# Output projection with eleven matmuls a tile in place of twelve, its weights brought into pieces of 128 rows by DMAs

## The chip, the core and the metric

The kernel runs on one core of a Trainium2 chip. The core has engines that run side by side, each with its own order of instructions and semaphores between them: TensorE (PE; its weight loads, PEld, run beside its matmuls), VectorE (DVE), ScalarE (ACT), GpSimd (POOL), and SyncE (SP), which here only issues DMAs. SBUF is the working memory of 128 partitions; PSUM takes what PE writes, in 8 banks of 128 x 512 float32.

The metric is the time of one execution on the device in microseconds, as the median of several runs. Beside it stands one profiled execution, whose trace gives each instruction's start and length.

## The reference

One block of a transformer with two parts, for a sequence of 2048 tokens with 448 channels, in float32. The first part is linear attention with 16 heads of 28 channels, the second an MLP over the tokens. Both are modulated by six vectors made from `c`.

```python
def _A_ref(x, wqkv, wo):
    q, k, v = qkv[0], qkv[1], qkv[2]                  # (x @ wqkv) cut into heads
    phi = lambda t: jnp.where(t > 0, t + 1, jnp.exp(t)) + 1e-6
    pq, pk = phi(q), phi(k)
    kv = jnp.einsum("bhsd,bhse->bhde", pk, v)
    z = jnp.einsum("bhsd->bhd", pk)
    num = jnp.einsum("bhqd,bhde->bhqe", pq, kv)
    den = jnp.einsum("bhqd,bhd->bhq", pq, z)[..., None] + 1e-6
    return (num / den).reshape(B, S, D) @ wo          # after turning the heads back

h = _layernorm(x) * (1 + ca) + sa
x = x + ga * _A_ref(h, A_wqkv, A_wo)
h = _layernorm(x) * (1 + cb) + sb
x = x + gb * _B_ref(h, B_w1, B_b1, B_w2, B_b2)        # W2 gelu(W1 h) over tokens
```

The output projection of the title is `num / den @ wo`. The kernel never forms `num`: it multiplies the masked `kv`, `wo` and `ga` into one 448 x 448 matrix Wp, so that a tile's result is phi(q), divided by its denominators, times Wp.

## The kernel before

The sequence is cut into 16 tiles of 128 tokens (`NT`). Products that must keep float32 accuracy are made from two parts: a value is copied on ACT into a rounded format (float32r; the "high" part) and the rest is subtracted on DVE (the "low" part). A product is then three matmuls, high x high, high x low and low x high. `split` (lines 78 to 80) is this pair of operations.

The kernel has these stages. First k and the outer products of phi(k) with the normalised x are made for all tiles, with some of the q projections between them (`Q_EARLY`: tiles 0 to 4). Then Wp is made (lines 846 to 852). Then comes the loop of lines 856 to 916, which is the stage of the change. Then the rest of the MLP's first matrix product, and the second one.

The loop has NT + LAG = 21 passes. Pass `i` issues, in a pipeline over the tiles:

- on PE: the transposes of tile i (`b_transpose`, line 763), the output projection of tile i-1 (`b_out`, line 776), the q projections that are left (`a_q`, 11 matmuls each; their number a pass stands in `QS`, else one), and from pass 5 on the first MLP product of tile i-5 (`step`, 12 matmuls)
- on ACT and DVE: the high and low part of the turned tile (`b_high`, `b_low`; on the trace pth and ptl), the residual sum of tile i-2 (`b_res`), the scaled phi(q) of tile i+1 (`b_prod`, `b_sum`, `b_recip`, `b_scale`; on the trace pd, den and pn, which the next pass turns), the second layer norm of tiles i-3 and i-4 (y, and the parts h2h and h2l that `step` multiplies), then phi of the q tiles projected in the pass before (`a_phi_q`; eq and rq on ACT, pq on DVE)
- splits of pieces of the first MLP matrix, ahead of their use (`split_to`; on the trace ph and pl from the raw piece pr), and their loads (`load_to`)
- on POOL: the small operations of the layer norm (nm, ny, vw, rt, nb), the addition in the denominators, and the low part of four of the weight pieces as accumulating DMAs (`PIECE_DMA`)

Each engine works in the order in which the program issues to it; nothing is reordered by a planner. A pool of tiles (`slot`, `tslot`, `bank`) makes a new tile wait until an older one in the same place is done with.

The 448 channels of phi(q) are turned in four groups of 112 (`G`, four heads). So Wp, too, lies in four pieces of 112 rows, and PE makes each as the product of a group of `kvm` and a piece of `wo` into a bank (`wp`); `split` makes their parts `Wph` and `Wpl` from there. `b_out` then has four groups with three matmuls each, over 112 rows.

Of the kernel before, what the change touches and what calls it, by code (L numbers as in the profile page):

```python
# [8 lines left out]
F32 = mybir.dt.float32  # L9
F32R = mybir.dt.float32r  # L10
AF = mybir.ActivationFunctionType
# [3 lines left out]
P = 128  # L15
S, D, F = 2048, 448, 1792
NT = S // P
NF = F // P
G = 112
# [15 lines left out]
LAG = 5  # L35
LAST, CUT = 2, 224
MOD_AT = {9: [(4, 0)], 10: [(4, 1)], 11: [(4, 2)], 12: [(4, 3)], 13: [(3, 0)], 14: [(3, 1)]}
QS = {0: 2, 4: 2}
WARM = 9
PRE = 9  # L40
MID = 5
# [6 lines left out]
def block_kernel(ctx: ExitStack, tc: tile.TileContext, x, xt, wqkv, wo, w1, b1, w2, b2, c, wmod, wfirst, out):  # L48
    nc = tc.nc
# [15 lines left out]
    def slot(name, w=D, dt=F32, parts=P):  # L65
        return slots.tile([parts, w], dt, name=name, tag="slot", padded_shape=[P, 512])

    def tslot(name, dt=F32, parts=P, w=D):
        return tok.tile([parts, w], dt, name=name, tag="tok", padded_shape=[P, 512])


    def moving(new, name, dt=F32R, parts=P):
        return new(name, dt=dt, parts=parts, w=512)[:, 16:16 + D]

    def bank(name):
        return psum.tile([P, 512], F32, name=name, tag="bank")

    def split(full, hi, lo):
        nc.scalar.activation(hi, full, AF.Copy)  # L79
        nc.vector.tensor_sub(lo, full, hi.bitcast(F32))  # L80
# [6 lines left out]
    ident = cst.tile([P, P], F32, name="ident")  # L87
# [44 lines left out]
    def load_mod(j):  # L132
        for k in range(4):
            wm[j, k] = (tslot if j == 5 else slot)(f"wm{j}_{k}", parts=G)
            nc.sync.dma_start(wm[j, k], wmod[k * G:(k + 1) * G, j * D:(j + 1) * D])
# [55 lines left out]
    def mod_out(j, ps):  # L191
        mods[j] = cst.tile([P, D], F32, name=f"mod{j}")
        nc.scalar.activation(mods[j], ps[:, :D], AF.Copy, bias=1.0 if j == 4 else 0.0)
# [35 lines left out]
    def mod_part(j, k):  # L229
        if k == 0:  # L230
            macc[j] = (tslot if j == 5 else slot)(f"acc{j}", parts=G)
            nc.vector.tensor_scalar_mul(macc[j], wm[j, 0], sc[:G, 4:5])
        else:
            nc.vector.scalar_tensor_tensor(macc[j], wm[j, k], sc[:G, 4 + k:5 + k], macc[j], op0=ALU.mult, op1=ALU.add)


    def mod_split(j):
        acc = macc.pop(j)
        macc[j] = (moving(slot, f"mh{j}", parts=G), moving(slot, f"ml{j}", parts=G))
        split(acc, *macc[j])  # L240

    def mod_sum2(j):
        ps = bank(f"modp{j}")
        hi, lo = macc.pop(j)
        nc.tensor.matmul(ps[:, :D], ones_r[:G, :], hi, start=True, stop=False)
        nc.tensor.matmul(ps[:, :D], ones_r[:G, :], lo, start=False, stop=True)
        return ps
# [45 lines left out]
    raws, parts = {}, {}  # L293
# [10 lines left out]
    def split_to(i):  # L304
        while done["split"] < min(i, len(pieces)):
            k = done["split"]
            n = pieces[k][3]
            if k in TOKP:
                hi, lo = tslot(f"ph{k}", F32R, w=n * P), tslot(f"pl{k}", F32R, w=n * P)
            else:  # L310
                hi, lo = slot(f"ph{k}", n * P, F32R), slot(f"pl{k}", n * P, F32R)
            if k in PIECE_DMA:
                full = raws.pop(k)
                nc.scalar.activation(hi, full, AF.Copy)
                nc.scalar.activation(lo, hi.bitcast(F32), AF.Copy, scale=-1.0)
                nc.gpsimd.dma_start(lo, full, accum_op=ALU.add)
            else:
                split(raws.pop(k), hi, lo)
            parts[k] = (hi, lo)
            done["split"] += 1  # L320
# [64 lines left out]
    tps = {}  # L385
# [55 lines left out]
    def phi_q(ps, t):  # L441
        dst, e, r = slot(f"pq{t}"), slot(f"eq{t}"), slot(f"rq{t}")
        nc.scalar.activation(e, ps, AF.Exp, scale=mv[t][:, 2:3])
        nc.scalar.activation(r, ps, AF.Relu, scale=mv[t][:, 2:3])
        nc.vector.scalar_tensor_tensor(dst, e, 1.0, r, op0=ALU.min, op1=ALU.add)
        return dst
# [4 lines left out]
    def a_q(t):  # L451
        project(t, 0, "qp")
        qps[t] = close(t, 0)
        del heads[t]

    def a_phi_q(keep=0):
        for t in sorted(qps)[:len(qps) - keep]:
            pq[t] = phi_q(qps.pop(t), t)
# [151 lines left out]
    for t in range(4, NT):  # L610
# [12 lines left out]
        if t == 12:  # L623
            mp = mod_sum2(2)
# [93 lines left out]
    mp = mod_sum2(4)  # L718
    kvb = bank("kvb")
    for ch in range(4):  # L720
        for g in range(4):
            s = slice(g * G, (g + 1) * G)
            nc.tensor.matmul(kvb[:G, s], raw_w[2, ch][:, s], csum[ch][:, s], start=(ch == 0 and g == 0),
                             stop=(ch == 3), skip_group_check=True)
# [4 lines left out]
    mp = mod_sum2(3)  # L729
    load_to(PRE + MID + 3)  # L730
    split_to(8)
    Wph, Wpl = [], []


    H2h, H2l = [None] * NT, [None] * NT
    pns, phs, ys, opb, sums, nms, nm2s, rss, vss = {}, {}, {}, {}, {}, {}, {}, {}, {}
# [11 lines left out]
    def b_eps(t):  # L748
        nc.gpsimd.tensor_scalar_add(dens[t], dens[t], 1e-6)
# [13 lines left out]
    def b_transpose(t):  # L763
        pn = pns.pop(t)
        tps[t] = bank(f"tq{t}")
        for g in range(4):
            nc.tensor.transpose(tps[t][:G, g * P:(g + 1) * P], pn[:, g * G:(g + 1) * G], ident)  # L767

    def b_high(t):
        phs[t] = (slot(f"pth{t}", 512, F32R, parts=G), slot(f"ptl{t}", 512, F32R, parts=G))  # L770
        nc.scalar.activation(phs[t][0], tps[t][:G, :], AF.Copy)  # L771

    def b_low(t):
        nc.vector.tensor_sub(phs[t][1], tps.pop(t)[:G, :], phs[t][0].bitcast(F32))

    def b_out(t):
        ph, pl = phs.pop(t)
        opb[t] = bank(f"op{t}")
        n = 0
        for g in range(4):  # L780
            s = slice(g * P, (g + 1) * P)
            for a, b in ((ph, Wph[g]), (ph, Wpl[g]), (pl, Wph[g])):
                nc.tensor.matmul(opb[t][:, :D], a[:, s], b, start=(n == 0), stop=(n == 11))  # L783
                n += 1

    def b_sums(i):
        if i not in vss:
# [42 lines left out]
    def b_low2(t):  # L830
        nc.vector.tensor_sub(H2l[t], ys.pop(t), H2h[t].bitcast(F32))
# [6 lines left out]
    def step(k, accs, mh, ml, first, last):  # L838
        hi, lo = parts.pop(k)
        for i, ps in enumerate(accs):  # L840
            acc3(ps, hi, lo, slice(i * P, (i + 1) * P), mh, ml, first, last)
# [4 lines left out]
    for g in range(4):  # L846
        wp = bank(f"wp{g}")
        nc.tensor.matmul(wp[:G, :D], kvm[:, g * G:(g + 1) * G], wo_sb[g], start=True, stop=True)
        hi, lo = moving(tslot, f"wph{g}", parts=G), moving(tslot, f"wpl{g}", parts=G)
        split(wp[:G, :D], hi, lo)  # L850
        Wph.append(hi)
        Wpl.append(lo)
    mod_out(3, mp)

    accs, early = None, []
    for i in range(NT + LAG):
        if i == NT - 4:
            load_mod(5)
        if NT - 3 <= i <= NT:
            mod_part(5, i - NT + 3)  # L860
        if i == NT:
            mod_split(5)
        if i < NT:
            b_transpose(i)
        if 0 <= i - 1 < NT:
            b_out(i - 1)
        nq = min(len(late), QS.get(i, 1))
        for _ in range(nq):
            a_q(late.pop(0))
        t = i - LAG  # L870
        mp = mod_sum2(5) if i == NT else None
        if t >= 0:
            if t == 0:
                accs = [bank(f"up{f}") for f in range(4)]
            if i > NT:
                if not early:
                    early = [bank(f"up{W1G[1][0] + f}") for f in range(W1G[1][1])]
                r = i - NT - 1
                step(NT + r, early, H2h[r], H2l[r], r == 0, False)
            step(t, accs, H2h[t], H2l[t], t == 0, t == NT - 1)  # L880
        if mp is not None:
            mod_out(5, mp)
        if i < NT:
            b_high(i)
        scale, res, norm1, norm2 = i + 1 < NT, 0 <= i - 2 < NT, 0 <= i - 3 < NT, 0 <= i - 4 < NT
        if res:
            b_res(i - 2)
        if scale:
            b_prod(i + 1)
        if norm2:  # L890
            b_norm2(i - 4, i)
        if res:
            b_mean1(i - 2, i)
        if norm1:
            b_norm1_a(i - 3)
        if scale:
            b_sum(i + 1)
        if norm1:
            b_norm1_b(i - 3, i)
        if scale:  # L900
            b_eps(i + 1)
        if i < NT:
            b_low(i)
        if norm1:
            b_mean2(i - 3, i)
        if scale:
            b_recip(i + 1)
        if scale:
            b_scale(i + 1)
        if norm2:  # L910
            b_low2(i - 4)
        a_phi_q(nq)
        load_to(14 + (i + 1) // 2)
        split_to(10 + (i + 1) // 2)
        if res or norm1:
            b_rstd(i, 0 if res else 1, 2 if norm1 else 1)

# [248 lines left out]
    for o0, n in W1G[1:]:  # L1166
# [5 lines left out]
        for r in range(first, NT):  # L1172
# [4 lines left out]
            if xleft and k % 2:  # L1177
                t = xleft.pop(0)
# [13 lines left out]
    for n, (kind, p) in enumerate(order):  # L1192
        if jobs:
            jobs.pop(0)()
        while xleft:
            t = xleft.pop(0)
# [73 lines left out]
```

## Time and profile before

| | |
|---|---|
| median of 3 runs | 447.32 us (446.92 to 447.51) |
| profiled execution, whole | 448.35 us |
| its span in the profile | 446.2 us |
| PE busy | 439.1 us, 98% |
| DVE busy | 353.5 us, 79% |
| ACT busy | 267.5 us, 60% |
| POOL busy | 104.3 us, 23% |
| granted clock of PE | 1.0 |
| first transposes of the loop (tile 0) | at 117.43 us |
| last transposes of the loop (tile 15) | at 199.96 us |

How to read its lines: a line of the order of time has the start in us, the length in us, the engine, the line of the kernel, the operation, what it writes and what it reads, the shapes, and the count where several are merged. In brackets stands how long the engine had idled before it and what ended the idle time. PE's matmuls overlap, so what one costs is the distance between two starts, not its length; the same holds to a smaller degree for DVE and ACT. A row of DMAs has the queue that issues, the count, the size of each and the time from issue to landing. `wp`, `op` and `tq` are the banks of Wp's product, of the output projection and of the transposes.

### The profile page before, as it was taken

The numbers are of one execution on the slowest core, as the hardware profiler recorded it, in microseconds if no ns is written. First come the engines' busy times: TensorE is split into PE (matmuls) and PEld (weight loads), VectorE is DVE, ScalarE is ACT, GpSimd is POOL, SyncE is SP. The second block draws the span as 40 slices with busy tenths as digits, with TensorE's granted clock in tenths as the row PEclk, the third lists the DMA queues.
The fourth block names the chain that finished last, engine by engine and source line by source line (L and its number), as shares of the span: only waits on it lengthen the run. The fifth ranks groups of instructions, "written<-read, shape, count | busy, mean of one in ns | idle before, by whom it ended". The sixth has DMA issues, their size and how long they took to land.

```text
span 446.2 us, 7331 instructions
## 1 busy us (share of the span) xinstructions
PE 439.1 (98%) x2370; PEld 405.5 (91%) x2370; DVE 353.5 (79%) x801; ACT 267.5 (60%) x580; POOL 104.3 (23%) x188
## 2 busy tenths in 40 slices
PE   7999999999999999999999999999999999999997
PEld 6878899999899999989999999999999999999996
DVE  3989997689998899896477776649688787978873
ACT  3899877748656876667664345336554546356531
POOL 3227563300025355554300000000110211302101
PEclk9999999999999999999999999999999999999999
DMA  7997999545100004222416453227987569966334
GB/s 236 378 303 165 215 241 229 104 147 181 54 0 1 24 25 114 54 48 47 143 54 217 137 178 127 90 88 228 257 201 194 92 177 214 208 183 110 54 89 62
DMA packets 58853, 63.22 MB, mean 142 GB/s; under 512 B 5248, under 2 KB 49344, under 8 KB 58816
## 3 DMA queue, kind: packets, MB, share of 16 engines
q1 hardware_dynamic: 51616, 51.17, 38.0%
q0 software_dynamic: 7200, 11.60, 16.4%
q8 instruction: 18, 0.29, 0.3%
q14 instruction: 19, 0.16, 0.1%
HBM read 46.57 MB, written 7.34 MB: 121 GB/s over the span
## 4 chain that ended last, share of the span: by engine, by line
PE 91%; ACT 3%; DVE 2%; POOL 1%; DMA 1%; issue 1%; SPq 0%; ACTq 0%
PE y L1026 14%; PE up L836 10%; PE up L835 10%; PE up L834 9%; PE cacc L512 7%; PE qp L418 7%; PE op L783 7%; PE y L1027 7%; PE kp L418 6%; PE yp L834 2%; PE yp L836 2%; PE yp L835 2%; PE tq L767 1%; DMA xt<-in_xt_dram 1%; PE qp L425 1%
## 5 line engine op out<-in xcount | busy, mean ns | idle before, releaser
L836 PE MATMUL up<-h2h,pl 128*128 128x448 f32 x224 | 81.4, 363 | 0.0
L835 PE MATMUL up<-h2l,ph 128*128 128x448 f32 x224 | 81.2, 362 | 0.0
L834 PE MATMUL up<-h2h,ph 128*128 128x448 f32 x224 | 80.8, 361 | 0.0
L80 DVE TENSOR_TENSOR pl<-pr,ph 128x512 fp32r<-128x512 f32 (+1 forms) x60 | 36.3, 616 | 14.2 <-ACT ph L79 9.9
L79 ACT ACTIVATE ph<-pr 128x512 fp32r<-128x512 f32 (+1 forms) x60 | 33.0, 570 | 24.0 <-PE up L835 17.7
L835 PEld LDWEIGHTS up<-h2l,ph 128*128 128x128 f32 x224 | 42.1, 188 | 3.1
L834 PEld LDWEIGHTS up<-h2h,ph 128*128 128x128 f32 x224 | 41.9, 187 | 3.0
L836 PEld LDWEIGHTS up<-h2h,pl 128*128 128x128 f32 x224 | 42.1, 188 | 2.4
L988 POOL DMA_DIRECT2D a<-a x12 | 10.9, 952 | 113.8 <-DMA a<-in_B_w_dram 101.7
L1046 POOL DMA_DIRECT2D out_dram<-yt x12 | 10.5, 874 | 82.3 <-DVE yt L1037 53.9
L512 PE MATMUL cacc<-pkh,xh 128*128 128x448 f32 x64 | 24.4, 381 | 0.3 <-ACT pkh L486 0.3
L783 PE MATMUL op<-wph,pth 112*128 112x448 f32 x64 | 24.5, 382 | 0.0
L418 PE MATMUL kp<-wh,hh 128*128 128x448 f32 x64 | 23.2, 373 | 1.1 <-ACT wh L253 1.1
L1032 ACT ACTIVATE cc<-y 128x448 f32<-128x448 f32 x18 | 9.8, 545 | 23.4 <-PE y L1027 20.4
L512 PE MATMUL cacc<-pkl,xh 128*128 128x448 f32 x64 | 23.3, 364 | 0.2 <-DVE pkl L488 0.2
L418 PE MATMUL qp<-wh,hh 128*128 128x448 f32 x64 | 23.3, 364 | 0.0
L783 PE MATMUL op<-wpl,pth 112*128 112x448 f32 x64 | 23.2, 363 | 0.0
L783 PE MATMUL op<-wph,ptl 112*128 112x448 f32 x64 | 23.2, 362 | 0.0
L834 PE MATMUL yp<-uw,qw 128*128 128x448 f32 x54 | 19.9, 368 | 0.0
L771 ACT ACTIVATE pth<-tq 112x512 fp32r<-112x512 f32 x16 | 9.6, 599 | 17.1 <-PE tq L767 17.1
L836 PE MATMUL yp<-uw,qw 128*128 128x448 f32 x54 | 19.7, 364 | 0.0
L835 PE MATMUL yp<-uw,qw 128*128 128x448 f32 x54 | 19.6, 364 | 0.0
(241 smaller groups left out, 1308.9 us busy)
## 6 DMA issues: line engine op xcount, KB each, us to landing
pr<-in_B_w_dram SPq DMA_DIRECT2D x48, 256.0 KB, 3.0
a<-in_B_w_dram SPq DMA_DIRECT2D x24, 256.0 KB, 4.9
a<-in_B_w_dram SPq DMA_DIRECT2D x24, 192.0 KB, 4.9
xt<-in_xt_dram SPq DMA_DIRECT2D x16, 256.0 KB, 4.9
x<-in_A_x_dram SPq DMA_DIRECT2D x16, 224.0 KB, 4.9
wm<-in_B_wmod_dram SPq DMA_DIRECT2D x16, 196.0 KB, 5.1
wr<-in_qkv_dram SPq DMA_DIRECT2D x12, 224.0 KB, 5.3
out_dram<-x SPq DMA_DIRECT2D x12, 224.0 KB, 2.0
```

Source lines behind the costliest of these rows:

```text
L79: nc.scalar.activation(hi, full, AF.Copy)
L80: nc.vector.tensor_sub(lo, full, hi.bitcast(F32))
L418: nc.tensor.matmul(pps[t, j][:, :D], a[:, ch * P:(ch + 1) * P], w, start=first, stop=False)
L512: nc.tensor.matmul(cacc[ch][:, :D], a[:, s], b, start=(t == 0 and i == 0), stop=(t == NT - 1 and i == len(todo) - 1))
L783: nc.tensor.matmul(opb[t][:, :D], a[:, s], b, start=(n == 0), stop=(n == 11))
L834: nc.tensor.matmul(ps[:, :D], hi[:, sl], mh, start=first, stop=False)
L835: nc.tensor.matmul(ps[:, :D], hi[:, sl], ml, start=False, stop=False)
L836: nc.tensor.matmul(ps[:, :D], lo[:, sl], mh, start=False, stop=last)
L988: nc.gpsimd.dma_start(w, a, accum_op=ALU.add)
L1026: nc.tensor.matmul(ps[:, :D], h[:, s], w, start=opens and r == 0, stop=False, skip_group_check=True)
L1027: nc.tensor.matmul(ps[:, :HD], l[:, s], wh, start=False, stop=closes and r == PAIRS - 1, skip_group_check=True)
L1046: nc.gpsimd.dma_start(of[t * P:(t + 1) * P, :], ysum.pop(t), accum_op=ALU.add)
```

## The change

Phi(q) is turned in three pieces of 128 channels, and the last 64 channels twice. A transpose of channels 320 to 447 fills the fourth block of the bank; a further one of channels 384 to 447 overwrites its first 64 rows. So rows 0 to 63 and rows 64 to 127 of that block hold the same 64 channels. `b_out` has three matmuls for each of three pieces. For the last 64 channels it has two: one with the high part of phi(q), which stands there twice, against a piece that holds the high part of Wp in its first 64 rows and the low part in the other 64, and one with 64 rows of low part against the high part. That is eleven matmuls, and five transposes.

Wp is still made in groups of 112 rows. ACT copies each group out of its bank (`wpg`). Eight DMAs on the SP queue bring the rows into four pieces of 128 (`wpr`), the last 64 rows twice. The split of these pieces (`wp_split`) stands inside pass 0 of the loop, behind the scaled phi(q) of tile 1.

Two counts move with it. `QS` gives three q projections to pass 0 and one to each pass from 1 to 5 (before: two to pass 0 and to pass 4, one to passes 1, 2, 3 and 5). `split_to` puts pieces 8, 9 and 10 of the MLP matrix into passes 1, 2 and 3 (before: 8 and 9 in pass 0, 10 in pass 1); piece 11 stays in pass 3.

```diff
-QS = {0: 2, 4: 2}
+QS = {0: 3}
...
     def b_transpose(t):
         pn = pns.pop(t)
         tps[t] = bank(f"tq{t}")
-        for g in range(4):
-            nc.tensor.transpose(tps[t][:G, g * P:(g + 1) * P], pn[:, g * G:(g + 1) * G], ident)
+        for ch in range(3):
+            nc.tensor.transpose(tps[t][:, ch * P:(ch + 1) * P], pn[:, ch * P:(ch + 1) * P], ident)
+        nc.tensor.transpose(tps[t][:, 384:], pn[:, 320:D], ident)
+        nc.tensor.transpose(tps[t][:64, 384:], pn[:, 384:D], ident)
...
     def b_high(t):
-        phs[t] = (slot(f"pth{t}", 512, F32R, parts=G), slot(f"ptl{t}", 512, F32R, parts=G))
-        nc.scalar.activation(phs[t][0], tps[t][:G, :], AF.Copy)
+        phs[t] = (slot(f"pth{t}", 512, F32R), slot(f"ptl{t}", 512, F32R))
+        nc.scalar.activation(phs[t][0], tps[t], AF.Copy)
...
-        n = 0
-        for g in range(4):
-            s = slice(g * P, (g + 1) * P)
-            for a, b in ((ph, Wph[g]), (ph, Wpl[g]), (pl, Wph[g])):
-                nc.tensor.matmul(opb[t][:, :D], a[:, s], b, start=(n == 0), stop=(n == 11))
-                n += 1
+        todo = []
+        for ch in range(3):
+            s = slice(ch * P, (ch + 1) * P)
+            todo += [(ph[:, s], Wph[ch]), (ph[:, s], Wpl[ch]), (pl[:, s], Wph[ch])]
+        todo += [(ph[:, 384:], Wph[3]), (pl[:64, 384:], Wph[3][:64])]
+        for n, (a, b) in enumerate(todo):
+            nc.tensor.matmul(opb[t][:, :D], a, b, start=(n == 0), stop=(n == len(todo) - 1))
...
     for g in range(4):
         wp = bank(f"wp{g}")
         nc.tensor.matmul(wp[:G, :D], kvm[:, g * G:(g + 1) * G], wo_sb[g], start=True, stop=True)
-        hi, lo = moving(tslot, f"wph{g}", parts=G), moving(tslot, f"wpl{g}", parts=G)
-        split(wp[:G, :D], hi, lo)
+        wpg = tslot(f"wpg{g}", parts=G)
+        nc.scalar.activation(wpg, wp[:G, :D], AF.Copy)
+        if g == 0:
+            Wpr += [tslot(f"wpr{ch}") for ch in range(4)]
+        for ch in range(4):
+            r0, r1 = max(ch * P, g * G), min(ch * P + P, (g + 1) * G)
+            for p0 in (0, 64) if ch == 3 else (0,):
+                if r0 < r1:
+                    nc.sync.dma_start(Wpr[ch][p0 + r0 - ch * P:p0 + r1 - ch * P], wpg[r0 - g * G:r1 - g * G])
+    mod_out(3, mp)
+
+    def wp_split(ch):
+        hi = moving(tslot, f"wph{ch}")
         Wph.append(hi)
-        Wpl.append(lo)
-    mod_out(3, mp)
+        if ch < 3:
+            Wpl.append(moving(tslot, f"wpl{ch}"))
+            split(Wpr[ch], hi, Wpl[ch])
+        else:
+            nc.scalar.activation(hi, Wpr[3], AF.Copy)
+            nc.vector.tensor_sub(hi[64:], Wpr[3][64:], hi[64:].bitcast(F32))
...
+        if i == 0:
+            for ch in range(4):
+                wp_split(ch)
         a_phi_q(nq)
         load_to(14 + (i + 1) // 2)
-        split_to(10 + (i + 1) // 2)
+        split_to(8 + i if i < 3 else 10 + (i + 1) // 2)
```

More of the change, by code (lines that the diff above doesn't have):

```diff
@@ L731, in block_kernel @@
     split_to(8)
-    Wph, Wpl = [], []
+    Wpr, Wph, Wpl = [], [], []
     H2h, H2l = [None] * NT, [None] * NT
@@ L765, in b_transpose @@
         tps[t] = bank(f"tq{t}")
-        for g in range(4):
-            nc.tensor.transpose(tps[t][:G, g * P:(g + 1) * P], pn[:, g * G:(g + 1) * G], ident)
+        for ch in range(3):
+            nc.tensor.transpose(tps[t][:, ch * P:(ch + 1) * P], pn[:, ch * P:(ch + 1) * P], ident)
+        nc.tensor.transpose(tps[t][:, 384:], pn[:, 320:D], ident)
+        nc.tensor.transpose(tps[t][:64, 384:], pn[:, 384:D], ident)
     def b_high(t):
-        phs[t] = (slot(f"pth{t}", 512, F32R, parts=G), slot(f"ptl{t}", 512, F32R, parts=G))
-        nc.scalar.activation(phs[t][0], tps[t][:G, :], AF.Copy)
+        phs[t] = (slot(f"pth{t}", 512, F32R), slot(f"ptl{t}", 512, F32R))
+        nc.scalar.activation(phs[t][0], tps[t], AF.Copy)
     def b_low(t):
-        nc.vector.tensor_sub(phs[t][1], tps.pop(t)[:G, :], phs[t][0].bitcast(F32))
+        nc.vector.tensor_sub(phs[t][1], tps.pop(t), phs[t][0].bitcast(F32))
     def b_out(t):
```

## The prediction

> **What bounds the kernel now.** I read the page first (busy times, then the shares of the chain that ended last), then what TensorE (PE) waited for, then busy time by stretch, then the order of time around the changed lines.
>
> ```profile
> span 446.2 us, 7331 instructions
> PE 439.1 (98%) x2370; PEld 405.5 (91%) x2370; DVE 353.5 (79%) x801; ACT 267.5 (60%) x580; POOL 104.3 (23%) x188
> ...
> PE 91%; ACT 3%; DVE 2%; POOL 1%; DMA 1%; issue 1%; SPq 0%; ACTq 0%
> ...
> L80 DVE TENSOR_TENSOR pl<-pr,ph 128x512 fp32r<-128x512 f32 (+1 forms) x60 | 36.3, 616 | 14.2 <-ACT ph L79 9.9
> ```
>
> PE is the bound of the whole: 98% busy and 91% of the chain. By that alone every matmul that goes is a gain. The stage of the change, the loop of sixteen tiles, says something else. The next rows are PE's only wait between 100 and 230 us, and two stretches of the loop (length; busy PE, PEld, DVE, ACT, POOL; clock; DMA share; GB/s).
>
> ```profile
> PE tq L767 <- DVE pn L756: 0.2, 1, 0.2
> ...
> 157.00:170.00 13.00, 13.00 (x72) 12.08 (x71) 12.82 (x29) 8.40 (x19) 7.15 (x15) 1.00 0.08 21
> 170.00:200.00 30.00, 29.78 (x159) 27.39 (x158) 27.22 (x64) 20.89 (x45) 15.30 (x35) 1.00 0.35 80
> ```
>
> VectorE (DVE) is busy 12.82 of 13.00 us there and PE does wait for it once. The loop has two bounds lying on each other: PE, and the elementwise work that feeds it.
>
> **What PE gains.** The first rows are one tile of the loop on PE.
>
> ```profile
> 157.29 0.36 PE L836 MATMUL up<-h2h,pl 128*128 128x448 f32 x1
> 157.29 0.55 PEld L767 LDWEIGHTS tq<-ident,pn 128*112 128x112 f32 x4
> 157.49 0.60 PE L767 MATMUL tq<-ident,pn 128*112 128x128 f32 x4
> 157.85 0.45 PE L783 MATMUL op<-wph,pth 112*128 112x448 f32 x1
> 158.13 0.36 PE L783 MATMUL op<-wpl,pth 112*128 112x448 f32 x1
> 158.33 0.36 PE L783 MATMUL op<-wph,ptl 112*128 112x448 f32 x1
> ```
>
> Matmuls start 0.20 us apart (158.13 to 158.33), so twelve to eleven frees 0.20 us a tile. Without the four transposes the second op matmul would start 0.40 after the last up matmul, at 157.69; it starts at 158.13, so four transposes cost 0.44, or 0.11 each. The fifth costs between 0.06 (only half a tile wide, the others no dearer) and 0.16 (the weight loads, 0.55 for 448 columns, grown to 576). I take 0.44 x 128/448 = 0.13, which scales the measured cost by columns. PE's net gain is 0.07 us a tile, 16 x 0.07 = 1.1 us in the loop (0.6 to 2.2 by the ends).
>
> The Trainium skill, "TensorE: Matmul & The Clock Gate", section "LDWEIGHTS (loading the stationary operand)", says that a load costs by its columns and not by its rows. By it the eleventh matmul, with 64 rows, is no cheaper, and the transposes go by columns; a price per transpose would give 16 x (0.20 - 0.11) = 1.4 us instead of 1.1. No row here has a 64-column load.
>
> **The way of Wp.** The four pieces leave PSUM as before (four ACT copies), but the DVE subtracts move behind eight DMAs. The rows: ACT's first and last copy, DVE's four subtracts, the SP queue before and after (three issues, then none until 152), four issues at the kernel's start, and times to landing.
>
> ```profile
> 115.37 0.54 ACT L79 ACTIVATE wph<-wp 112x448 fp32r<-112x448 f32 x1 [2.27 <-PE wp L848]
> 117.63 0.55 ACT L79 ACTIVATE wph<-wp 112x448 fp32r<-112x448 f32 x1 [0.21 <-PE wp L848]
> 116.83 2.21 DVE L80 TENSOR_TENSOR wpl<-wp,wph 112x448 fp32r<-112x448 f32 x4
> 118.50 0.60 ACT L771 ACTIVATE pth<-tq 112x512 fp32r<-112x512 f32 x1
> 109.61 2.03 SPq L301 DMA_DIRECT2D pr<-in_B_w_dram  x3
> 152.43 0.33 SPq L301 DMA_DIRECT2D pr<-in_B_w_dram  x1
> 1.23 1.84 SPq L149 DMA_DIRECT2D wm<-in_first_dram  x4
> xpark<-x SPq DMA_DIRECT2D x4, 224.0 KB, 1.9
> pr<-in_B_w_dram SPq DMA_DIRECT2D x16, 128.0 KB, 2.3
> c_sb<-in_c_dram SPq DMA_DIRECT2D x1, 4.0 KB, 1.7
> pk<-pk POOLq DMA_DIRECT2D x11, 224.0 KB, 5.2
> ```
>
> SP is free from 111.6 to 152.4, so the eight issues meet nothing ahead; behind them stands a weight load that was not let go before 152.4. An issue takes 1.84/4 = 0.46. The last copy ends at 118.18, and the three DMAs that read it go at about 118.6, 119.0 and 119.5. No row has a plain SBUF to SBUF transfer; its ends are 1.7 (4 KB) and 5.2 us (accumulating, on the POOL queue). I take 1.9, the SP row that starts in SBUF. The last piece lands at 121.4, the first ones earlier, and ACT, which comes out of pth at 119.0, ends its four copies at about 122.0. DVE follows with its four subtracts at 122.75, the delayed q tile (eq, rq, pq) ends at 123.7, and the two operations that come next in DVE's order (0.6 each) by 124.9. PE meanwhile has three q projections in place of two (33 matmuls instead of 22) and asks for Wp only at 125.2. So the DMAs cost PE nothing; the cover is that third projection, 11 x 0.20 = 2.2 us. Without it PE would ask at 123.0, when all pieces are just there. Four more copies on ACT and the 128-row forms of pth and ptl cost nothing on the path: ACT is busy 8.40 of 13.00 us in this stage, and these operations go by elements per row (0.60 for 112x512, 0.62 mean for 128x512).
>
> **What the third projection does to DVE.** The rows are, in order of time, PE's turns, the q operations on ACT, and DVE where it waited for ACT.
>
> ```profile
> 122.29 0.60 PE L767 MATMUL tq<-ident,pn 128*112 128x128 f32 x4
> 122.92 0.60 ACT L771 ACTIVATE pth<-tq 112x512 fp32r<-112x512 f32 x1 [1.74 <-PE tq L767]
> 123.42 0.63 ACT L443 ACTIVATE eq<-qp,mv 128x448 f32<-128x448 f32 x1
> 124.97 0.66 ACT L444 ACTIVATE rq<-qp,mv 128x448 f32<-128x448 f32 x1
> 124.48 0.68 DVE L774 TENSOR_TENSOR ptl<-tq,pth 112x512 fp32r<-112x512 f32 x1
> 136.45 0.63 DVE L445 SCALAR_TENSOR_TENSOR pq<-eq,rq 128x448 f32<-128x448 f32 x1 [0.88 <-ACT rq L444]
> 137.49 0.60 PE L767 MATMUL tq<-ident,pn 128*112 128x128 f32 x4
> 141.28 0.62 DVE L756 SCALAR_TENSOR_TENSOR pn<-pq,den 128x448 f32<-128x448 f32 x1
> 142.79 0.63 DVE L445 SCALAR_TENSOR_TENSOR pq<-eq,rq 128x448 f32<-128x448 f32 x1 [0.34 <-ACT rq L444]
> 144.76 0.60 PE L767 MATMUL tq<-ident,pn 128*112 128x128 f32 x4
> 149.63 0.63 DVE L445 SCALAR_TENSOR_TENSOR pq<-eq,rq 128x448 f32<-128x448 f32 x1 [1.45 <-ACT rq L444]
> 150.69 0.62 DVE L445 SCALAR_TENSOR_TENSOR pq<-eq,rq 128x448 f32<-128x448 f32 x1 [0.42 <-ACT rq L444]
> 157.11 0.63 DVE L445 SCALAR_TENSOR_TENSOR pq<-eq,rq 128x448 f32<-128x448 f32 x1 [0.43 <-ACT rq L444]
> ```
>
> 1. The second tile's transposes move from 122.29 to 122.29 + 2.2 + 0.13 = 124.6, its pth (0.76 later, 0.63 before plus the fifth transpose) to 125.4, its ptl to 126.0 instead of 124.48. DVE waits about 1.1 us there, from 124.9, having nothing else in its order.
> 2. From that ptl to the sixth tile's pn DVE took 141.28 - 124.48 = 16.8 us. In the changed order the same stretch holds one pq more and two weight splits more (pieces 8 and 9, put off by the new split count): 0.53 (a step in the row of four, (2.21 - 0.62)/3) + 2 x 0.60. Also the third pq must wait for its rq: six ACT operations of 0.52 (three steps from 123.42 to 124.97) behind pth end at 129.1, where DVE is ready at 128.6: 0.45. Together 19.0: pn starts at 145.0, ends at 145.6.
> 3. PE's turn without the second projection in the fifth pass comes at 144.76 + 0.13 - 0.28 = 144.6: the 2.2 us are given back, and four passes gain 0.07 each. PE must wait for pn, until 145.8: a stall of 1.2 us (0.7 to 1.6, if the 0.45 and the wait of 1.1 are off).
> 4. From pn at 141.28 to the last pq at 157.11 were 15.8 us. One pq falls out (0.53), and the waits of 0.34, 1.45, 0.42 and 0.43 become some 0.2, 0.4 and 0.4, like the last, where one q is done: 2.2 less, 13.6. The last pq starts at 158.6, 1.5 later than before.
>
> **What follows to the end of the loop.**
>
> ```profile
> 175.59 0.71 DVE L807 SCALAR_TENSOR_TENSOR y<-y,rt,mod 128x448 f32<-128x448 f32 x1 [0.72 <-POOL rt L819]
> ...
> 199.19 0.63 DVE L756 SCALAR_TENSOR_TENSOR pn<-pq,den 128x448 f32<-128x448 f32 x1
> ...
> 199.96 0.62 PE L767 MATMUL tq<-ident,pn 128*112 128x128 f32 x4 [0.22 <-DVE pn L756]
> ```
>
> From 157 on DVE runs without a pause, then waits for POOL (row at 175.59), which waits for DVE and ACT: a ring that does not ask PE for anything, and that PE meets at 199.96. It moves as a whole by 1.5, so PE's last transposes are at 201.5. PE gains nothing on the way: it waits at pn again and again. After them two projections remain with 0.20 less each, and 0.13 more for these transposes: 1.5 + 0.13 - 0.40 = +1.2 us at the end of the loop. The rest is PE's alone and moves with it. Against the profiled execution (span 446.2, 448.35 us in all) this is 449.6; that execution stands 1.03 above the median, so I forecast 447.32 + 1.2 = **448.5 us**. Own range 447.9 to 449.3 (the stall's ends, and 0.16 for the transposes).
>
> **The rivals.**
> - PE sets the end everywhere: the ring has more slack than I read. Then 16 x 0.07 = 1.1 comes off: 446.2. It decides if pn of the sixth tile ends before 144.4. DVE would have to lose both its 0.45 and the repeated 0.88 (row at 136.45), since without any wait it would end at about 144.3. For it: 98% PE. Against: the wait at 199.96.
> - The stall comes but the ring takes up most of it, where ACT idles behind POOL: half of 1.2 minus the last two tiles, about 447.6, within noise.
> - The DMAs land late, as the 5.2 us row: the last at 124.7, ACT and DVE two microseconds later in the second tile (ptl at 128.2 instead of 126.0): 448.5 + 2.2 = 450.7. Against: that row accumulates through another queue.
> - In that rival the wait before the sixth tile grows to 3.4 us. The Trainium skill, "TensorE: Matmul & The Clock Gate", section "What's actually happening", has the clock fall to half after an idle window of about 3.4 us; an estimate by it is 1.7 us more, 452.4. The granted clock stays at 1.00 in both stretches shown; no run here has such a gap.
>
> **How the numbers follow.** My forecast 0.62, PE alone 0.12, taken up 0.20, late DMAs 0.04, these with the clock 0.02. A measurement of this kernel tells about 0.2%, 0.9 us, from no change: 446.4 and 448.2 are the bounds. Faster is the second case, 0.12; the same is the third and the lower edge of mine, 0.24; slower 0.64. The range 446.4 to 450.0 leaves out the late DMAs and most of the case of PE alone.
>
> **What would show it.** Right: PE waits for pn of about 1 us near 144.5 and more near 190 to 201; DVE idle about 1 us near 125; the eight DMAs landed by 122; twelve op matmuls gone to eleven at 0.20 apart. Wrong: no PE wait in the loop, or one at the op matmuls for Wp (then the way of Wp is on the path), or transposes far from 0.57 a tile.

## The result, and the profile after

| | before | after |
|---|---|---|
| median of 6 runs | 447.31 us (446.56 to 448.34) | 451.47 us (451.11 to 452.5) |
| profiled execution, whole | 448.35 us | 451.61 us |
| its span | 446.2 us | 449.9 us |

The changed kernel takes 1.01 times as long (95% interval 1.0088 to 1.0112). The forecast was 448.5 us with a range of 446.4 to 450.0: the sign was right, the time is 3.0 us over it and outside the range, and the mechanism behind it is another one.

The page of the changed kernel, its span, busy times and the shares of the chain that ended last:

```profile
span 449.9 us, 7348 instructions
...
PE 444.3 (99%) x2370; PEld 403.8 (90%) x2370; DVE 353.9 (79%) x801; ACT 269.3 (60%) x584; POOL 103.6 (23%) x188
...
PE 95%; DVE 1%; ACT 1%; DMA 1%; SPq 0%; issue 0%; DVEq 0%; ACTq 0%
```

PE is busy 5.2 us longer than before with as many instructions (one matmul a tile less, one transpose more), and its share of the chain grew from 91% to 95%. What PE waited for, in the whole execution, in order of size (us in total, times, longest):

```profile
PE warm L178 <- DVE roots L101: 1.1, 1, 1.1
PE cacc L512 <- ACT pkh L486: 0.3, 1, 0.3
PE rw L391 <- DVE rowst L383: 0.3, 1, 0.3
```

None of these is in the loop. The 0.22 us for pn that stood there before is gone, and the wait of 1.2 us that the prediction puts before the sixth tile has not come. PE became slower by itself. The order of time shows where; the next rows are the turn of one tile on PE, and then the weight loads (PEld) at its end:

```profile
158.74 0.49 PE L767 MATMUL tq<-ident,pn 128*128 128x128 f32 x3
159.06 0.27 PE L768 MATMUL tq<-ident,pn 128*128 128x128 f32 x1
159.17 0.27 PE L769 MATMUL tq<-ident,pn 128*64 128x128 f32 x1
159.20 0.45 PE L787 MATMUL op<-wph,pth 128*128 128x448 f32 x1
159.49 0.36 PE L787 MATMUL op<-wpl,pth 128*128 128x448 f32 x1
...
160.89 0.36 PE L787 MATMUL op<-wph,ptl 128*128 128x448 f32 x1
161.09 0.37 PE L787 MATMUL op<-wph,pth 128*128 128x448 f32 x1
161.38 0.46 PE L787 MATMUL op<-wph,ptl 64*128 64x448 f32 x1
161.78 0.47 PE L837 MATMUL up<-h2h,ph 128*128 128x448 f32 x1
162.09 0.36 PE L838 MATMUL up<-h2l,ph 128*128 128x448 f32 x1
...
160.89 0.19 PEld L787 LDWEIGHTS op<-wph,pth 128*128 128x128 f32 x1
161.38 0.18 PEld L787 LDWEIGHTS op<-wph,ptl 64*128 64x128 f32 x1 [0.30 <-issue]
161.77 0.19 PEld L837 LDWEIGHTS up<-h2h,ph 128*128 128x128 f32 x1 [0.21 <-issue]
```

Starts are 0.20 us apart up to 161.09. Then they are 0.29, 0.40 and 0.31 apart, until 162.09: 1.00 us for three steps in place of 0.60, so 0.40 to 0.41 a tile. The steps lie around the eleventh matmul, the one with 64 rows. The loads say the same: normally one starts while the matmul ahead of it runs (160.89, with the matmul at 160.89). The load of the 64 rows starts together with its own matmul (161.38), after 0.30 us in which no load ran, and so does the next one, the return to 128 rows. Sixteen tiles of 0.41 are 6.6 us. Against the kernel before, 0.20 of it comes back with the twelfth matmul, and the fifth transpose adds 0.11, so a tile should be about 0.32 us longer.

The tiles' transposes, in the rows of the sixth, eighth, ninth and last tile, begin 5.55 to 5.57 us apart from the seventh on (158.74 to 164.29), where they were 5.25 to 5.27 apart (the row at 157.49 before, and the next at 162.74):

```profile
145.32 0.55 PE L767 MATMUL tq<-ident,pn 128*128 128x128 f32 x3
...
158.74 0.49 PE L767 MATMUL tq<-ident,pn 128*128 128x128 f32 x3
164.29 0.49 PE L767 MATMUL tq<-ident,pn 128*128 128x128 f32 x3
...
203.22 0.49 PE L767 MATMUL tq<-ident,pn 128*128 128x128 f32 x3
```

From the first to the last of these transposes PE takes 86.60 us (116.62 to 203.22) where it took 82.53 (117.43 to 199.96). Fourteen of the fifteen distances hold an output projection. So 14 x 0.31 + 0.11, less the 0.39 by which the last distance before was longer than the others, gives 4.06: the 4.07 that was measured. Of the 3.7 us between the spans, these are +4.07; what follows the last transposes is +0.44 (two projections are left there); and the loop begins 0.81 earlier. The last belongs to the profiled execution of before, not to the change. PE waited there near the start of the kernel (total, times, longest):

```profile
PE kp L418 <- ACT wh L253: 1.1, 1, 1.1
PE col L215 <- DVE acc L208: 0.6, 1, 0.6
```

In the changed kernel both are 0.2. In the executions below, whatever their code in the loop, the loop began between 116.2 and 117.3 us. So times on the clock of two traces are compared from the loop's first transposes on.

### The profile page after: what moved, and what is told of

Its sections match the earlier page's. It is cut to its first block, busy times and chain, and to the rows that moved or that the text cites. A ratio compares the mean times of both kernels' runs of the same rounds, so it can differ in the third digit from the quotient of the medians.

```text
span 449.9 us, 7348 instructions
## 1 busy us (share of the span) xinstructions
PE 444.3 (99%) x2370; PEld 403.8 (90%) x2370; DVE 353.9 (79%) x801; ACT 269.3 (60%) x584; POOL 103.6 (23%) x188
## 4 chain that ended last, share of the span: by engine, by line
PE 95%; DVE 1%; ACT 1%; DMA 1%; SPq 0%; issue 0%; DVEq 0%; ACTq 0%
PE y L1048 14%; PE up L837 10%; PE up L838 10%; PE up L839 10%; PE op L787 9%; PE cacc L512 7%; PE qp L418 7%; PE y L1049 7%; PE kp L418 6%; PE yp L837 2%; PE yp L838 2%; PE yp L839 2%; PE tq L767 1%; DMA wm<-in_first_dram 1%; PE qp L425 1%; PE kvb L723 1%
## 5 line engine op out<-in xcount | busy, mean ns | idle before, releaser
L837 PE MATMUL up<-h2h,ph 128*128 128x448 f32 x224 | 82.4, 368 | 0.0
L787 PE MATMUL op<-wph,ptl 128*128 128x448 f32 x64 | 24.8, 387 | 0.0
L787 PE MATMUL op<-wph,pth 128*128 128x448 f32 x64 | 24.6, 384 | 0.0
L773 ACT ACTIVATE pth<-tq 128x512 fp32r<-128x512 f32 x16 | 9.6, 598 | 18.4 <-PE tq L769 18.4
L749 POOL TENSOR_SCALAR den<-den 128x16 f32<-128x16 f32 x16 | 7.7, 479 | 49.2 <-DVE den L746 49.0
```

Source lines behind the costliest of these rows:

```text
L787: nc.tensor.matmul(opb[t][:, :D], a, b, start=(n == 0), stop=(n == len(todo) - 1))
L837: nc.tensor.matmul(ps[:, :D], hi[:, sl], mh, start=first, stop=False)
```

## The experiments

Two theories stood against each other. The theory of the 64 rows: what was lost is the step down to 64 rows and back. The theory of the ring, from the prediction: the elementwise work of DVE, ACT and POOL sets the end of the loop. They can both hold, one above the other. The kernel before, which ran beside them, had medians between 447.23 and 447.37 us.

### All 128 rows in the last matmul

```diff
-        todo += [(ph[:, 384:], Wph[3]), (pl[:64, 384:], Wph[3][:64])]
+        todo += [(ph[:, 384:], Wph[3]), (pl[:, 384:], Wph[3])]
```

> The changed kernel with one edit: the eleventh matmul takes all 128 rows of the last block (both copies of the low part against high and low of Wp, which adds low x low, a term of the exact product) in place of 64 rows. Theory 64: in the changed kernel the starts around the 64-row matmul are 0.30, 0.40 and 0.31 us apart in place of 0.20, so 0.41 us a tile goes; the tile on TensorE falls from 5.56 to 5.15 us. If TensorE then sets the end alone, 451.5 - 16 x 0.41 = 444.9. Theory ring (my prediction's): the gain stops where the elementwise work of VectorE, ScalarE and GpSimd is late, with a TensorE wait for pn of about 2 us before the sixth tile's transposes, at 448 to 449. Rival rows (the number of rows has nothing to do with it; the DMA way of Wp or the fifth transpose is what costs): 451.5.

Measured: 448.82 us, 1.0035 times the kernel before (1.0021 to 1.0048). Its profiled execution was the shortest of five, 448.13 us; the others took 448.75 to 449.05. Its chief wait on PE, with the first and the last place of it:

```profile
PE tq L767 <- DVE pn L756: 2.3, 3, 1.2
...
144.80 0.55 PE L767 MATMUL tq<-ident,pn 128*128 128x128 f32 x3 [1.24 <-DVE pn L756]
...
200.50 0.52 PE L767 MATMUL tq<-ident,pn 128*128 128x128 f32 x3 [0.60 <-DVE pn L756]
```

Where PE waits for nothing, the tiles are now 5.16 us apart (transposes at 152.22 and 157.38), 0.40 less than in the changed kernel and 0.09 less than before. And there, below PE, lies the ring as the prediction has it: a wait of 1.24 us before the sixth tile (the expectation had about 2), others near 189 and at 200.50. So 64 rows hold a slower bound above the one that was forecast. They cost 6.6 us of PE's time, but taking them away gives only about 2.6 us of the whole (451.47 to 448.82), because the ring then sets the end: in this trace PE's turns come some 3 us late in all, of which 2.3 are the waits that the profile names.

### 64 rows in the kernel before

```diff
             for a, b in ((ph, Wph[g]), (ph, Wpl[g]), (pl, Wph[g])):
+                if n == 11:
+                    a, b = a[:64], b[:64]
                 nc.tensor.matmul(opb[t][:, :D], a[:, s], b, start=(n == 0), stop=(n == 11))
```

> The kernel before with one edit: the last of the twelve matmuls of each tile takes 64 of its 112 rows (48 channels of a low part are left out of the output). No DMA way, no fifth transpose, the old counts. Theory 64: TensorE's tile grows by 0.41 us, less the 0.39 us that TensorE waited near 200: 447.3 + 6.6 - 0.4 = 453.5, and TensorE waits for nothing in the loop. Rival rows: 447.3.

Measured: 453.47 us, 1.0139 (1.0125 to 1.0153). Its rows, around the cut:

```profile
161.61 0.36 PE L785 MATMUL op<-wpl,pth 112*128 112x448 f32 x1
161.90 0.47 PE L785 MATMUL op<-wph,ptl 64*128 64x448 f32 x1
162.30 0.47 PE L836 MATMUL up<-h2h,ph 128*128 128x448 f32 x1
162.61 0.36 PE L837 MATMUL up<-h2l,ph 128*128 128x448 f32 x1
```

The same 0.29, 0.40, 0.31. Nothing else of the change is in this kernel, so the cost belongs to the 64 rows and not to the new order, the DMAs or the doubled rows.

### Two matmuls of 64 rows in a row

```diff
-        todo += [(ph[:, 384:], Wph[3]), (pl[:64, 384:], Wph[3][:64])]
+        todo += [(ph[:, 384:], Wph[3]), (pl[:64, 384:], Wph[3][:64]), (pl[:64, 384:], Wph[3][:64])]
```

> The changed kernel with the 64-row matmul issued twice in a row (its small term counts twice in the output). If the cost lies in going from 128 rows to 64 and back, the second one adds only its own 0.20 us: 451.5 + 16 x 0.20 = 454.7. If each 64-row matmul costs the extra 0.41 us by itself, 451.5 + 16 x 0.61 = 461.2. Rival rows gives 454.7 too, so this run tells only the two forms of theory 64 apart.

Measured: 454.95 us, 1.0171 (1.0157 to 1.0185). The rows:

```profile
162.10 0.36 PE L787 MATMUL op<-wph,pth 128*128 128x448 f32 x1
162.39 0.68 PE L787 MATMUL op<-wph,ptl 64*128 64x448 f32 x2
163.00 0.47 PE L837 MATMUL up<-h2h,ph 128*128 128x448 f32 x1
163.31 0.36 PE L838 MATMUL up<-h2l,ph 128*128 128x448 f32 x1
```

From 162.10 to 163.31 are 1.21 us, where one such matmul took 1.00: the second costs 0.21, the normal step. What is paid is leaving and coming back, once a tile.

### 80 and 32 rows

```diff
-                    a, b = a[:64], b[:64]
+                    a, b = a[:80], b[:80]      # the other kernel: [:32]
```

> The kernel before with the last of the twelve op matmuls cut to 80 of its 112 rows (it leaves out 32 channels of the last low part). With 64 rows the same cut cost 0.41 us a tile. Theory A (what costs is going down to a smaller form of the array, which holds 64 rows or fewer, and 98 rows were free): 80 rows are free, starts 0.20 us apart, time 447.3 us. Theory B (the cost grows as rows fall away, and 98 rows were only near enough to 128): starts 0.25 to 0.35 apart around it, time 449 to 452 us.

> The same cut to 32 rows (80 channels of the last low part left out). Theory A with one price for leaving and coming back: as with 64 rows, 0.41 us a tile, 453.5 us. Theory B (the cost grows as rows fall away): more than 0.41 us a tile, 454.5 us or more. If the cost is one for moving only half the rows, 32 rows would be dearer than 64 too.

Measured: with 80 rows 447.35 us, 0.9999 (0.9989 to 1.0008); with 32 rows 453.18 us, 1.0134 (1.0119 to 1.0149). The groups of the cut matmul and its load (busy us, mean ns), first of the kernel with 80 rows:

```profile
L785 PE MATMUL op<-wph,ptl 80*128 80x448 f32 x16 | 5.9, 367 | 0.0
L785 PEld LDWEIGHTS op<-wph,ptl 80*128 80x128 f32 x16 | 3.0, 188 | 0.2
```

And of the one with 32:

```profile
L785 PE MATMUL op<-wph,ptl 32*128 32x448 f32 x16 | 7.4, 465 | 0.0
L785 PEld LDWEIGHTS op<-wph,ptl 32*128 32x128 f32 x16 | 2.9, 181 | 4.8 <-issue 4.8
```

It is a step and not a slope: 80 rows are free, 32 cost what 64 cost, and both loads last as long as any (181 and 188 ns). The loads are not longer; they lose their overlap: 4.8 us of idle time in sixteen tiles ahead of them, 0.30 a tile, which the 80 rows don't have. The Trainium skill, "TensorEngine Tiling (Array Packing)", section "Available Configurations", lists forms of the array with 128, 64 and 32 rows, and its section "Key Properties" says that a change of the form drains TensorE. The traces fit that: the lost overlap stands on both sides of the cut matmul, and the price is 0.41 us for one way there and back. That a matmul of 64 rows is run in such a form is argued from the step between 80 and 64 rows; no trace names the form.

### The splits of the MLP's pieces ahead of those of Wp

To the kernel with 128 rows in the last matmul:

```diff
         if i == 0:
+            split_to(10)
             for ch in range(4):
                 wp_split(ch)
...
-        split_to(8 + i if i < 3 else 10 + (i + 1) // 2)
+        split_to(10 + (i + 1) // 2)
```

> The kernel with all 128 rows, and the splits of pieces 8 and 9 (two operations on ScalarE and two on VectorE) put back into pass 0, ahead of the splits of Wp, where VectorE waits 1.01, 0.58, 0.57 and 0.56 us for the DMAs and ScalarE. Theory ring: 1.2 us less VectorE work between the second and the sixth tile, so the end comes 1 us earlier than with full rows alone, near 447.3. If TensorE alone sets the end there, no difference from the run with full rows.

Measured: 447.64 us, 1.0008 (0.9999 to 1.0017). The wait before the sixth tile is gone (its transposes begin at 144.47 without one); the later ones stay, 1.0 us in two places. The rows that explain them are the accumulating DMA of a weight piece and `rt` on POOL, DVE's `y`, and PE; the last row is all that DVE waits for `rt` between 130 and 200 us:

```profile
184.71 0.95 POOL L316 DMA_DIRECT2D pl<-pr  x1 [3.00 <-ACT pl L315]
...
186.01 0.72 POOL L822 TENSOR_TENSOR rt<-vw,mhalf 128x2 f32<-128x2 f32 x1
...
186.76 0.71 DVE L810 SCALAR_TENSOR_TENSOR y<-y,rt,mod 128x448 f32<-128x448 f32 x1 [1.32 <-POOL rt L822]
...
189.05 0.52 PE L767 MATMUL tq<-ident,pn 128*128 128x128 f32 x3 [0.45 <-DVE pn L756]
...
DVE y L810 <- POOL rt L822: 2.6, 3, 1.3
```

So the 1.2 us before the sixth tile hung on pieces 8 and 9, which were put off (two subtracts of 0.60): done while DVE waits for the DMAs of Wp, they cost PE nothing there. The time fell by 1.2 us, to 447.64; the expectation was 447.3.

### The old counts, without the third projection

To the kernel with 128 rows, both counts as before (`QS = {0: 2, 4: 2}`, `split_to(10 + (i + 1) // 2)`).

> The changed kernel with the last matmul over all 128 rows and both counts as before (two q projections in passes 0 and 4, pieces 8 and 9 of the MLP matrix in pass 0). If the third projection of pass 0 is the cover of the way of Wp, as the prediction has it, PE now asks for Wp 2.2 us earlier, near 122.0 us, and waits for its pieces, the last of which were made at 123.9 us in the changed kernel: waits of 1.5 to 3 us near the first op matmuls, and then 448.5 to 450 us. If the cover is not needed (the first matmuls ask for one piece at a time, and the pieces come in the same order), PE waits less than 0.5 us there and, without the third projection's stall near 145, the time is 446.5 to 447.5 us.

Measured: 449.93 us (449.36 to 451.5), 1.0047 (1.0032 to 1.0063). The rows are, in order: PE's first op matmul, ACT's last copy of Wp, PE's third tile with the op matmuls behind it, and two stretches (length; busy PE, PEld, DVE, ACT, POOL; clock; DMA share; GB/s).

```profile
122.71 0.45 PE L787 MATMUL op<-wph,pth 128*128 128x448 f32 x1
...
123.19 0.58 ACT L870 ACTIVATE wph<-wpr 128x448 fp32r<-128x448 f32 x1 [0.64 <-DMA wpr<-wpg]
...
129.33 0.55 PE L767 MATMUL tq<-ident,pn 128*128 128x128 f32 x3 [1.95 <-DVE pn L756]
...
130.85 0.58 PE L787 MATMUL op<-wph,pth 128*128 128x448 f32 x1
131.22 0.57 PE L787 MATMUL op<-wpl,pth 128*128 128x448 f32 x1
...
124.00:130.00 6.00, 4.05 (x23) 3.44 (x22) 5.50 (x11) 4.95 (x10) 0.25 (x1) 1.00 0.00 1
130.00:136.00 6.00, 6.00 (x24) 5.40 (x24) 5.93 (x14) 2.40 (x5) 2.12 (x5) 0.72 0.00 0
```

The first theory was right about the time and wrong about the place. PE asks for Wp at 122.71 and never waits for it, since the pieces come in the order in which they are used. It is ACT and DVE, each working in order, that stand behind the landings; the third tile's pn is late, and PE waits 1.95 us for that. The run does not tell what the missing projection does alone, since both counts moved: the splits of pieces 8 and 9, 1.2 us on DVE from 125.39 on, stand here behind those of Wp and ahead of that pn. In this execution the granted clock then fell to half (0.50 from 130.5 to 133.4, 0.72 in the mean of the stretch): matmuls are 0.37 apart from 130.48 to 133.47, 1.6 us more for ten of them. This execution took 451.5 us whole, with a granted clock of 0.996 in the mean of its span. The other three took 449.36, 449.37 and 450.5, with 1.0 each, so the clock fell in this one alone, and the 450.5 has another reason, which no trace shows.

### The small operations of the layer norm first

DVE's pauses at y come behind `rt` on POOL, which stands in POOL's queue behind an accumulating DMA that waits for ACT. This kernel has the splits first, as two experiments above, and:

```diff
-        load_to(14 + (i + 1) // 2)
-        split_to(10 + (i + 1) // 2)
         if res or norm1:
             b_rstd(i, 0 if res else 1, 2 if norm1 else 1)
+        load_to(14 + (i + 1) // 2)
+        split_to(10 + (i + 1) // 2)
```

> The changed kernel with the last matmul over all 128 rows, the splits of pass 0 ahead of those of Wp, and in each pass the small operations of the layer norm on GpSimd (vw, rt, nm, nb) issued ahead of the split of the MLP's weight piece, whose accumulating DMA stands on the same queue and waits for ScalarE. What is left of PE's waits in the kernel without this move is 1.0 us (0.45 near 189 us, 0.60 near 200 us). Theory (the ring of DVE, GpSimd and ScalarE sets these waits, and DVE's pauses of 0.5 to 1.3 us at y behind rt are part of it): the pauses shrink, PE waits for pn no more, time 446.0 to 446.7 us. Rival (the pauses at y are slack, the ring is held elsewhere): PE's waits stay at about 1.0 us and the time at 447.6.

Measured: 446.31 us, 0.9972 (0.9961 to 0.9984). DVE's waits for `rt` between 130 and 200 us, 2.6 us in three places without the move, are all gone, and with them PE's near 189 and 200. One wait is left in PE's list:

```profile
144.46 0.55 PE L767 MATMUL tq<-ident,pn 128*128 128x128 f32 x3 [0.52 <-DVE pn L756]
...
198.72 0.49 PE L767 MATMUL tq<-ident,pn 128*128 128x128 f32 x3
```

That wait stands at the time at which this tile began in the kernel without the move (144.47), though the loop here began 0.41 us earlier (116.75 and 117.16). DVE sets it still, and what sets DVE, by the traces' releasers, is the way of Wp: the fifth of the eight issues ends at 119.4 in both traces (it took 1.52 us here and 1.11 there), ACT's last copy of Wp begins on its landing at 123.07 here and at 123.08 there, and from then on DVE's rows stand at the same times in both, up to pn at 143.78, with one more wait on the way (0.87 for rq). That makes this 0.5 us a likely cost of the DMAs; no run moves them alone, so it is not shown. Beside it two turns begin 0.14 and 0.21 us late (162.35 and 167.72), right behind their pn.

The same move in the kernel before:

> The kernel before with the same move alone (the small operations of the layer norm ahead of the split of the weight piece). Before, PE waits for pn only once, 0.22 us near 200 us. Theory of the ring: that wait goes, time 447.0 us, at most 0.3 below the kernel before. Rival (the pauses at y matter for more than this wait): 446.5 or less. If the move helps as much here as in the changed kernel, the eleven matmuls have no part in the gain.

Measured: 447.05 us, 0.9991 (0.9982 to 1.0). PE waits for pn nowhere in the loop, and the gain is the 0.22 us of that wait, within what was measured. So most of the 1.0 us that the kernel above gains is from the change itself, once nothing takes its gain away: 446.31 against 447.05, 0.7 us, though the runs of the two overlap (445.83 to 446.76, 446.48 to 447.96). On PE the eleven matmuls are worth 16 x (0.20 - 0.11) = 1.4, of which 0.9 is lost in the three places above; 0.5 remains by this sum, against 0.7 measured. The version with eleven matmuls of full height, the splits first and the small operations first is faster than both kernels, 1.0 us (0.3%) below the one before.

## Why the prediction was wrong, and where it was right

**What PE gains** is the step that failed. It priced the twelfth matmul gone at 0.20 us, which is right, and took the new eleventh as "no cheaper" than the others. With its neighbours it is dearer by 0.41: 0.61 us instead of 0.20. The net is not 0.07 us gained a tile but 0.31 lost, 1.1 us gained in the sum against some 4.5 lost (4.07 and 0.44). The sentence behind that price was about the load, and the load did last as long as any other (183 ns against 188). What the price missed is the overlap: "0.20" is the distance between two matmuls of which the second one's load runs beside the first; the runs show that among matmuls of 80 to 128 rows, and not on the way to 64 or 32 rows and back. No row of before had a matmul of 64 rows between others, so its cost should have had a bound on both sides. The range had none for it.

The other term of the step, the fifth transpose, was right: from the first transposes to the second op matmul are 0.75 us (158.74 to 159.49), where four took 0.64. It is 0.11 instead of 0.13, the price of a transpose and not by its columns; its 64 columns bring no such loss.

**The way of Wp** was right in what matters to PE and late in its sizes. The rows of the changed kernel are the issues, ACT's first wait for a landing, the last copy, the last subtract, PE's first op matmul, and one of the transfers:

```profile
115.14 5.80 SPq L860 DMA_DIRECT2D wpr<-wpg  x8
120.34 0.58 ACT L79 ACTIVATE wph<-wpr 128x448 fp32r<-128x448 f32 x1 [1.58 <-DMA wpr<-wpg]
122.72 0.58 ACT L870 ACTIVATE wph<-wpr 128x448 fp32r<-128x448 f32 x1 [0.61 <-DMA wpr<-wpg]
123.33 0.62 DVE L871 TENSOR_TENSOR wph<-wpr,wph 64x448 fp32r<-64x448 f32 x1 [0.56 <-ACT wph L870]
124.26 0.45 PE L787 MATMUL op<-wph,pth 128*128 128x448 f32 x1
...
wpr<-wpg SPq DMA_DIRECT2D x1, 168.0 KB, 3.5
```

The eight issues took 0.73 us each in the mean (5.80/8; the median is 0.58, the longest 1.27) and not 0.46; the three issues at 109.61 that the prediction shows would have given 0.68. A landing took 2.0 to 3.5 and not 1.9. The subtracts end at 123.95 instead of 122.75, and, as the loop began 0.81 earlier, that is 2.0 late from its first transposes. PE asks for Wp at 124.26 without waiting. That the third projection is the cover is not shown for Wp: in the kernel without it, PE did not wait for Wp either. There it was pn that came late, with both counts moved. (The 0.62 that the prediction sets beside ACT's 0.60 is a row of DVE; the conclusion holds, as the changed kernel's pth over 128 rows takes 0.60.)

**What the third projection does to DVE** was right in where it ends and in part by luck. The second tile's ptl was put at 126.0 and stands at 126.11; the sixth tile's pn was to end at 145.6 and ends at 145.26. But the loop began 0.81 earlier than before, so ptl is 0.9 later than forecast and pn 0.5. The wait of DVE for pth that was to be there, 1.1 us near 125, has not come: the subtracts of Wp were late, and DVE came straight from its own work to ptl. From ptl to pn it took 18.53 us instead of 19.0, which is 16.8 + 0.53 + 1.20; the 0.45 for the third rq is missing. Two errors nearly cancel. The wait on PE that follows needs a PE that is there by 144.6. In the changed kernel PE comes at 145.3, as pn ends, and next to no wait is left. With 128 rows PE is faster, and the wait is there, 1.24 us, with 448.82 us for the whole. That is near the forecast of 448.5, for the kernel that the prediction had in mind.

**To the end of the loop** was right too, in the same kernel. With 128 rows the last transposes are at 200.50, 84.1 us from the first ones, 1.6 more than before; the step had 1.5. The ring did move as a whole: from the first transposes on, DVE's row that was at 175.59 before (176.14 there) and its last pn (199.73 for 199.19) are 1.6 later too.

**The rivals.** "PE sets the end everywhere" (0.12) is what happened, with another price: the ring had slack because PE had become slower, and not by pn ending before 144.4. That the DMAs land late, the last near 122.7 us and not by 122, cost PE nothing in this kernel; it made DVE late, as said above. The sign against itself that the prediction named, "no PE wait in the loop", is what the profile shows.

## What to carry to other kernels

Count a matmul by the distance to its neighbours, and ask whether it uses as many rows of the array as they do: one of 64 or 32 rows among larger ones cost two whole matmuls more here, while the same product over 128 rows, with a small further term in it, was free. Where two bounds lie on each other, a gain on one shows nothing before the other is moved too, and a loss on one hides what happened to the other; take the loss out to see it. Work that can be moved is cheaper where the engine waits anyway. When two traces are compared by the clock, set them to the same event first: here a start 0.8 us earlier hid that much of an error.

## What the runs showed of the hardware

- One step to 64 or 32 rows and back among matmuls of 112 or 128 rows, with 448 columns moving: 0.40 to 0.41 us. 80 rows: none. Weights of 64 columns (the fifth transpose): none, it costs 0.11 like the others. A second matmul of 64 rows behind the first: 0.21, the normal step.
- In one execution a wait of 1.95 us on PE was followed by some 3 us at half clock (0.37 us between starts instead of 0.20); the other three of that kernel have a mean clock of 1.0. A wait of 1.24 us, in the kernel with 128 rows, was not followed by it: the matmuls behind it are 0.20 apart. The prediction, which took from the Trainium skill, "TensorE: Matmul & The Clock Gate", section "What's actually happening", an idle window of about 3.4 us, gave this a place only behind a gap of 3.4. In the one trace with it, the fall came behind less than that; that the wait was its cause is not shown.
- Eight transfers between places in SBUF (28 to 196 KB) in the changed kernel: 5.80 us for the issues on SP (median 0.58, the fifth 1.27), 2.0 to 3.5 us to land.
